# Keys and queries of two batches loaded eight tokens to a partition, and what follows for their use

## The chip, the cores and the metric

The kernel runs on one core of a Trainium2 chip. The core has a matrix engine (TensorE, PE in the profile, with its weight loads as PEld), a vector engine (VectorE, DVE), a scalar engine (ScalarE, ACT), GpSimd (POOL) and a sync engine (SP) that here only issues transfers. Sixteen DMA engines move data. SBUF is the on-chip memory of 128 partitions, PSUM the one that matrix results go to. The metric is the device time of one execution in microseconds (us); lower is better.

## The reference

A sparse attention of 4 batches, 8 heads, 768 tokens and 64 numbers to a head, followed by two matrix products with a gated activation between them. Cut to what matters:

```python
k_sum = k.reshape(B, H, nb, block, D).max(axis=3)      # block = 32, nb = 24
v_sum = v.reshape(B, H, nb, block, D).mean(axis=3)
scores_l = scale * np.matmul(q, k.transpose(0, 1, 3, 2))
mask_l = np.abs(pos[:, None] - pos[None, :]) < window  # window = 16
scores_s = scale * np.einsum('bhsd,bhnd->bhsn', q, k_sum) + np.log(block)
a = softmax(np.concatenate([where(mask_l, scores_l, -1e9), scores_s], axis=-1))
x = np.matmul(a, np.concatenate([v, v_sum], axis=2))   # then heads side by side: 3072 x 512
h = x @ w_in                                           # 512 x 2048
out = (h / (1 + exp(-beta * h))) @ w_out               # 3072 x 512
```

A token thus looks at some 31 neighbours and at one summary (a maximum of keys, a mean of values) for each of 24 blocks.

## The kernel before

The order of work is written out by hand: every engine executes its instructions in the order of the program, and the planner is a small list in which "main" steps on TensorE have "side" steps set between them at given positions (`run`, with pairs of position and function). Batch 0 has a path of its own. For each of batches 1 to 3, the scores and the weighted sums are computed during the output product of the batch before, and the loads and layouts for it during the hidden product and the output product of the batch before.

The eight heads go in four pairs g. A pair's two heads lie in partitions 0 to 63 and 64 to 127 of the transposed tiles. For each batch and pair:

- `kT[g]`: keys transposed, 128 partitions (2 heads x 64 numbers) by tokens, with 16 zero columns at either end. `qn[g]`: queries in the same way, without the zeros.
- `kw[g]`: twelve windows, one for each tile of 64 queries, of 128 columns: 96 neighbouring keys, then the 24 block maxima. It is the stationary operand of the scores.
- `km[g]`: the block maxima, copied by POOL into each window (`key_sums`, L237).
- The scores (L307) take for every tile and head 64 query columns of `qn` as the moving operand. ScalarE makes the exponentials (L316), VectorE or POOL multiplies by the mask (L320), TensorE multiplies with values (L395), VectorE divides (L422), and ScalarE issues a DMA transpose of the result to `xT` (L447).

How keys and queries come into these layouts differs by batch. Batches 0 and 1 are loaded by POOL's queue with a cast to bf16, eight tokens to a partition (CS, L44), into `krow` and `qrow` (96 rows); TensorE transposes them (L256), and copies out of PSUM (L240, L243) put the tokens in order. There, block c of 96 columns holds the tokens 8r + c. For batch 1 the window copy (`windows_perm`, L216) reads with a step, and the maximum is taken from the windows (`key_max_win`, L228).

Batches 2 and 3 go another way, all issued by SP. `hw_load` (L87, DMA at L90) brings a pair's 384 KB of f32 into a staging tile, token 128 j + p in partition p, so that each packet is one token's 64 numbers, 256 B. POOL casts it to bf16 (`kq_cast`, L453 to L456) into a tile of a pool of its own, `natp`. SP issues a DMA transpose (`kq_dma`, L465 to L468) into `kT` or `qn`, tokens in order. VectorE then copies the windows from `kT` (`windows_nat`, L225) and takes the maximum from `kT` (`key_max_nat`, L232). The values take the same sort of way (`load_v`, L94; `v_cast`, L324; `v_odd_dma`, L335), and their block means come from a product with `A_avg` (`vm_all`, L369).

The positions of these steps are in the last loop of the kernel (L708 to L752). SP's queue holds, for a batch, in this order: two query loads (behind the stores of the output product that ends there), then key transposes with the other query loads between them, value loads, query transposes, the two DMAs per pair for the values, and the key loads for the next batch. An instruction in that queue that waits holds all behind it.

Of the kernel before, what the change touches and what calls it, by code (L numbers as in the profile page):

```python
# [11 lines left out]
def kernel(  # L12
# [10 lines left out]
    nc = tc.nc  # L23
    ctx.enter_context(tc.manual_schedule())
    P = 128
    f32 = mybir.dt.float32
    bf16 = mybir.dt.bfloat16
# [4 lines left out]
    B, H, S, D = q.shape  # L32
    block = 32
    W = 16
    nb = S // block
    QT = 64
    NT = S // QT
    HT = NT // 2
    HS = S // 2
    J6 = S // P  # L40
    JV = 2 * J6 + 1
    G = H // 2
    NK = QT + 2 * W
    CS = (8, 8)  # L44
    scale = 1.0 / math.sqrt(D)
    log_block = math.log(block)
    d_model = moe_w_in.shape[0]
# [6 lines left out]

    const = ctx.enter_context(tc.tile_pool(name="consts", bufs=1))
    stage = ctx.enter_context(tc.tile_pool(name="stage", bufs=4))
    natp = ctx.enter_context(tc.tile_pool(name="nat", bufs=4))
    ep = ctx.enter_context(tc.tile_pool(name="ep", bufs=8))
    xp = ctx.enter_context(tc.tile_pool(name="xp", bufs=4))
    op = ctx.enter_context(tc.tile_pool(name="op", bufs=3))  # L60
# [7 lines left out]
    def pair(a, b, g):  # L68
        return a[b, 2 * g:2 * g + 2]


    stg = {}
    loads = {}

    krow = const.tile([P, H // 2 * 16 * D], bf16, name="krow")
    qrow = const.tile([P, H // 2 * 16 * D], bf16, name="qrow")
    def row_view(t, b, lo, hi):
        c = CS[b]
        r = S // c
        hs = H // (2 if 2 * r <= P else 1)  # L80
        p0 = lo // hs * QT
        return t[p0:p0 + r].rearrange("p (h e) -> p h e", e=c * D)[:, lo % hs:lo % hs + hi - lo]

    def sw_load(t, src, b, lo, hi):
        return nc.gpsimd.dma_start(out=row_view(t, b, lo, hi), in_=src[b, lo:hi].rearrange("h (p c) d -> p h (c d)", c=CS[b]))

    def hw_load(nm, src, b, g):  # L87
        f = stage.tile([P, 2, J6, D], f32, name=nm + "st", tag=nm + "st")
        stg[(nm, b, g)] = f
        nc.sync.dma_start(out=f[:], in_=pair(src, b, g).rearrange("h (j p) d -> p h j d", p=P))  # L90

    vst = [const.tile([P, JV, D], f32, name=f"vst{g}") for g in range(G)]

# [38 lines left out]
    kw = [const.tile([P, NT, P], bf16, name=f"kw{g}") for g in range(G)]  # L132
# [3 lines left out]
    kT = [const.tile([P, S + 2 * W], bf16, name=f"kT{g}") for g in range(G)]  # L136
# [47 lines left out]
    qn = [const.tile([P, S], bf16, name=f"qn{g}") for g in range(G)]  # L184
# [28 lines left out]
    def strided(a, dims):  # L213
        return bass.AP(a.tensor, a.offset, [list(a.ap[0])] + dims)

    def windows_perm(cp, g, src, C):  # L216
        R, F, FW = S // C, QT // C, W // C
        t = kw[g][:, :, 0:NK].rearrange("p m (f c) -> p m f c", c=C)
        cs = src.ap[1][0]
        cp(t[:, 1:NT - 1], strided(src[:, :, F - FW:], [[F, NT - 2], [1, F + 2 * FW], [cs, C]]))  # L220
        e = kw[g][:, 0, W:NK]
        cp(strided(e, [[(NT - 1) * P - W, 2], [C, F + FW], [1, C]]),
           strided(src[:, :, 0:1], [[R - F - FW, 2], [1, F + FW], [cs, C]]))

    def windows_nat(cp, g):  # L225
        cp(kw[g][:, :, 0:NK], strided(kT[g][:, 0:1], [[QT, NT], [1, NK]]))

    def key_max_win(g):  # L228
        nc.vector.tensor_reduce(out=km[g][:, NK:NK + nb].rearrange("p (m n) -> p m n", n=2),  # L229
                                in_=kw[g][:, :, W:W + QT].rearrange("p m (n f) -> p m n f", f=block), op=ALU.max, axis=AX.X)  # L230

    def key_max_nat(g):  # L232
        nc.vector.tensor_reduce(out=km[g][:, NK:NK + nb], in_=kT[g][:, W:W + S].rearrange("p (n f) -> p n f", f=block),  # L233
                                op=ALU.max, axis=AX.X)
# [13 lines left out]
    def turned(row, b, t, g):  # L248
        C = CS[b]
        R = S // C  # L250
# [8 lines left out]
    def kt0(g, bg, cp, km=True):  # L259
        t = turned(krow, 0, big[bg], g)  # L260
        cp(kT[g][:, W:W + S].rearrange("p (f c) -> p f c", c=CS[0]), t.rearrange("p c f -> p f c"))
        if km:
            key_max_nat(g)

    def kt_pe(b, g, bg, cp):
        windows_perm(cp, g, turned(krow, b, big[bg], g), CS[b])

# [4 lines left out]
    def qt_pe(b, g, bg, cp):  # L272
        t = turned(qrow, b, big[bg], g)
        cp(qn[g].rearrange("p (f c) -> p f c", c=CS[b]), t.rearrange("p c f -> p f c"))


    et = {}

    def q_tile(g, h, m):
        return qn[g][h * D:(h + 1) * D, m * QT:(m + 1) * QT]  # L280

    def scores0(g, u, bg, pe=True):
        s = big[bg]
# [18 lines left out]
    def scores(b, g, u, bg):  # L302
        s = big[bg]
        for j in range(HT):
            m = u * HT + j
            for h in range(2):
                nc.tensor.matmul(s[:, h, j * QT:(j + 1) * QT], kw[g][h * D:(h + 1) * D, m, :], q_tile(g, h, m),  # L307
                                 start=True, stop=True)
        weigh(b, g, u, s)
        if g < G - 1 or b == 1:  # L310
            mask_e(b, g, u)
# [136 lines left out]
                                    in_=xn[(b, g)].rearrange("p j h d -> p (j h d)"))  # L448


    nat = {}

    def kq_cast(eng, nm, b, g):  # L453
        t = natp.tile([P, J6, 2, D], bf16, name=nm + "n", tag=nm + "n")
        nat[(nm, b, g)] = t
        return eng.tensor_copy(out=t[:], in_=stg[(nm, b, g)].rearrange("p h j d -> p j h d"))  # L456

    last_mask = {}

    def key_cast(n, g):  # L460
        i = kq_cast(nc.gpsimd, "k", n, g)
        if g == 0 and n - 1 in last_mask:
            behind(i, last_mask[n - 1])

    def kq_dma(nm, b, g):  # L465
        t = kT[g][:, W:W + S] if nm == "k" else qn[g][:]
        nc.sync.dma_start_transpose(out=t.rearrange("p (j t) -> p j t", j=J6),
                                    in_=nat[(nm, b, g)].rearrange("p j h d -> p (j h d)"))  # L468


    def h_begin(i, t, lo, hi):
# [150 lines left out]
    s = []  # L622
    wo = []

    def scale4(p, eng=None):
        for n in range(4 * p, 4 * p + 4):
            scale_w_out(n, eng)
# [26 lines left out]
    s = [(6, lambda: scale4(1)), (12, lambda: scale4(2)), (.5, clear_kw)]  # L654
# [5 lines left out]

    def load_keys(n):
        for g in range(G):
            hw_load("k", k, n, g)


    def scores_at(b, s, pos):
# [24 lines left out]
    s = [(.05, exp_table), (.15, lambda: scale4(3)), (.7, lambda: km_pe(2, nc.gpsimd)), (2.9, lambda: km_pe(3, nc.gpsimd))]  # L691
# [16 lines left out]
    for b in range(1, B):  # L708
        n = b + 1
        s = []  # L710
        if n < B:
            for g in range(2):
                s.append((0 + .1 * g, lambda g=g, n=n: hw_load("q", q, n, g)))
            for g in range(G):
                s.append((.5 + g, lambda g=g: key_cast(n, g)))
                s.append((.6 + g, lambda g=g: kq_dma("k", n, g)))
                s.append((3.5 + g, lambda g=g: windows_nat(dve_cp, g)))
                s.append((3.6 + g, lambda g=g: key_max_nat(g)))
                s.append((4.7 + g, lambda g=g: kq_cast(nc.gpsimd, "q", n, g)))
                s.append((8 + g, lambda g=g: key_sums(nc.gpsimd, g)))  # L720
                s.append((6.6 + 1.5 * g, lambda g=g: kq_dma("q", n, g)))
                s.append((12.6 + 1.2 * g, lambda g=g: v_cast(nc.gpsimd, g)))
                s.append((12.7 + 1.2 * g, lambda g=g: v_odd_dma(g)))
            for g in range(2):
                s.append((.7 + g, lambda g=g, n=n: hw_load("q", q, n, g + 2)))
                s.append((2.7 + g, lambda g=g: load_v(n, g)))
                s.append((6.7 + 1.5 * g, lambda g=g: load_v(n, g + 2)))
        if n + 1 < B:
            for g in range(G):
                s.append(((16.31, 16.32, 19.3, 19.31)[g], lambda g=g, n=n: hw_load("k", k, n + 1, g)))  # L730
        late = [x for x in s if x[0] >= 16]
        run([lambda i=i: h_tile(i) for i in range(k2)], [x for x in s if x[0] < 16])
        s = [((x[0] - 16) * 1.2, x[1]) for x in late]
        if n < B:
            scores_at(n, s, [1, 5.9, 8, 10.1])
            av_at(n, s, [10.2, 13.1, 13.2, 13.3], [0, 1, 2, 0])
            for g in range(G):
                s.append(((10.3, 13.35, 13.4, 13.5)[g], lambda g=g: x_dma(n, g)))
            s.append((5.99, lambda: vm_all(big[0], VMC)))
            s.append((6.3, lambda: spread(0)))  # L740
            s.append((8.3, lambda: spread(1)))
        main = [lambda ms=ms, a=a: o_atom(b, ms, a) for ms in range(J6 - (n == B)) for a in range(4)]
        run(main, s)
        if n == B:
            ms = J6 - 1
            for lo, hi in ((0, 256), (256, 512)):
                t = one[0 if lo else 1][:, 0]
                for kk in range(k2):
                    o_mm(ms, kk, t, lo, hi)
                o = op.tile([P, hi - lo], f32, name="o_half", tag=f"o_half{lo}", bufs=1)  # L750
                nc.vector.tensor_copy(out=o[:], in_=t[:, 0:hi - lo])
                nc.sync.dma_start(out=out_r[b * J6 + ms][:, lo:hi], in_=o[:])  # L752
# [29 lines left out]
```

## Time and profile before

| | |
|---|---|
| median of 3 runs | 216.02 us (215.3 to 217.65) |
| profiled execution | 217.07 us, its span 215.3 us |
| TensorE clock granted | 1.000 |
| TensorE busy | 207.2 us |
| VectorE, ScalarE, POOL busy | 99.1, 107.7, 57.5 us |
| DMA packets | 85287, of them 73728 under 512 B |
| key loads of batches 2 and 3 (8) | 384 KB each, 5.4 us to landing |
| query loads of batches 2 and 3 (8) | 384 KB each, 4.1 us to landing |
| key and query transposes (8 and 8) | 4.3 and 4.1 us to landing |
| hidden product for batch 1's x, with the loads for batch 2 | 78.2 to 98.8 us |
| output product, with the scores of batch 2 | 98.8 to 124.2 us |
| hidden product for batch 2's x, with the loads for batch 3 | 124.2 to 145.0 us |
| output product, with the scores of batch 3 | 145.0 to 170.3 us |

Times within the profile are counted from the first instruction of the profiled execution. A group of instructions is told by line, engine, operation, what it writes and reads, partitions by elements, and number; then its busy time in us and the mean of one in ns; then the idle time of its engine just before it, and what ended most of that idle time. Waits are told as who waited for whom: us in total, times, longest. The chain of waits is the chain of work that ended last, with start, length and what ran.

### The profile page before, as it was taken

What the parts mean: (1) busy time and instruction counts of PE and PEld (TensorE: products, weight loads), DVE (VectorE), ACT (ScalarE), POOL (GpSimd) and SP (SyncE); (2) the same over time, 40 slices, a digit from 0 to 9 for tenths busy, and PEclk for the clock granted to TensorE, in tenths of its full rate; (3) what the DMA queues carried; (4) which work ended last, traced back from release to release, by engine and by line L of the source; (5) the groups of instructions that cost most, each with busy time, mean ns of one, the idle gap of its engine ahead of it and who ended that gap; (6) DMA issues with size and microseconds to landing.
All of it is one profiled execution on the core that took longest, in us unless ns stands there. A gap on an engine that the chain in (4) does not pass through costs nothing.

```text
span 215.3 us, 5346 instructions
## 1 busy us (share of the span) xinstructions
PE 207.2 (96%) x2242; PEld 121.0 (56%) x2242; DVE 99.1 (46%) x233; ACT 107.7 (50%) x143; POOL 57.5 (27%) x91
## 2 busy tenths in 40 slices
PE   7789999999999999999999999999999999999993
PEld 7567756665546445665455455654564556654452
DVE  5567766597786612530599212422796200002121
ACT  2258595777676007776681046676660077650000
POOL 7946990010517403441105004433000000000000
PEclk9999999999999999999999999999999999999999
DMA  6999999999949999999699979999527400001212
GB/s 118 181 212 161 191 175 198 206 209 191 225 114 226 269 199 236 230 195 159 147 215 214 247 184 227 180 200 196 136 70 182 120 24 0 0 3 49 97 49 97
DMA packets 85287, 34.09 MB, mean 158 GB/s; under 512 B 73728, under 2 KB 82320, under 8 KB 85264
## 3 DMA queue, kind: packets, MB, share of 16 engines
q1 hardware_dynamic: 68192, 24.05, 55.3%
q0 software_dynamic: 7440, 7.34, 21.3%
q10 hardware_dynamic: 9632, 2.37, 7.6%
q8 instruction: 17, 0.28, 0.6%
q14 instruction: 6, 0.05, 0.1%
HBM read 27.37 MB, written 6.29 MB: 156 GB/s over the span
## 4 chain that ended last, share of the span: by engine, by line
PE 87%; DMA 6%; DVE 3%; issue 1%; ACT 0%; POOL 0%; POOLq 0%; DVEq 0%
PE one L505 36%; PE big L487 29%; PE big L473 5%; PE one L479 3%; DMA xT<-xn 3%; DMA krow<-in_k_dram 3%; PE big L256 3%; PE big L307 3%; PE big L395 2%; PE big L479 2%; DVE xn L422 1%; DVE qn L243 1%; PE big L294 1%; PE big L286 1%; PE big L369 1%
## 5 line engine op out<-in xcount | busy, mean ns | idle before, releaser
L505 PE MATMUL one<-w_out_sb,h_sb 128*128 128x512 bf16 (+1 forms) x400 | 86.3, 371 | 0.0
L500 ACT ACTIVATE h_sb<-big,beta_sb 128x768 bf16<-128x768 f32 x48 | 42.7, 901 | 52.5 <-PE big L487 52.5
L487 PE MATMUL big<-xT,w_in_sb 128*128 128x384 bf16 x384 | 63.0, 326 | 0.3 <-DMA xT<-xn 0.3
L505 PEld LDWEIGHTS <-h_sb 128*128 128x128 bf16 x400 | 37.8, 98 | 40.9 <-issue 0.2
L487 PEld LDWEIGHTS <-w_in_sb 128*128 128x128 bf16 x384 | 37.6, 98 | 25.6 <-issue 0.5
L243 DVE COPY o_sb<-one 128x512 f32<-128x512 f32 x20 | 13.8, 688 | 47.4 <-PE one L505 47.3
L316 ACT ACTIVATE e<-big,bias 128x768 bf16<-128x768 f32 x32 | 27.1, 899 | 7.5 <-PE big L307 4.9
L320 DVE TENSOR_TENSOR e<-e,mask 128x768 bf16<-128x768 bf16 x24 | 14.2, 618 | 19.0 <-ACT e L316 18.9
L325 POOL CAST ve<-vst 128x832 bf16<-128x832 f32 x15 | 13.2, 889 | 9.8 <-DMA vst<-in_v_dram 9.7
L243 DVE COPY kw<-kT 128x1152 bf16<-128x1152 bf16 x8 | 4.0, 496 | 22.5 <-DMA kT<-kn 22.5
L456 POOL CAST qn<-qst 128x768 bf16<-128x768 f32 x8 | 6.6, 830 | 28.7 <-DMA qst<-in_q_dram 28.7
L237 POOL COPY kw<-km 128x288 bf16<-128x288 bf16 x12 | 5.5, 471 | 27.6 <-DVE km L229 21.7
L422 DVE TENSOR_TENSOR xn<-big,r 128x768 bf16<-128x768 f32 (+1 forms) x14 | 12.6, 900 | 0.5
L233 DVE TENSOR_REDUCE km<-kT 128x24 bf16<-128x768 bf16 x12 | 11.2, 943 | 2.4 <-ACT kT L240 2.4
L473 PE MATMUL big<-xT,w_in_sb 128*128 128x384 bf16 x64 | 11.4, 326 | 0.0
L456 POOL CAST kn<-kst 128x768 bf16<-128x768 f32 x8 | 6.5, 828 | 13.8 <-DVE e L320 11.4
L620 ACT ACTIVATE h_sb<-big,beta_sb 128x384 bf16<-128x384 f32 x16 | 8.1, 580 | 2.7 <-PE big L473 2.7
L522 PE MATMUL one<-blank 128*128 128x128 bf16 (+1 forms) x105 | 7.2, 231 | 1.3 <-DVE blank L118 1.3
L479 PEld LDWEIGHTS <-w_in_sb 128*128 128x128 bf16 x64 | 6.1, 98 | 4.0
L479 PE MATMUL one<-xT,w_in_sb 128*128 128x384 bf16 x44 | 8.1, 326 | 0.0
L473 PEld LDWEIGHTS <-w_in_sb 128*128 128x128 bf16 x64 | 5.9, 98 | 3.5
L395 PEld LDWEIGHTS <-e 128*64 128x64 bf16 x336 | 6.2, 111 | 2.1 <-issue 1.6
(122 smaller groups left out, 187.8 us busy)
## 6 DMA issues: line engine op xcount, KB each, us to landing
out_dram<-o_sb SPq DMA_DIRECT2D x23, 256.0 KB, 2.5
vst<-in_v_dram SPq DMA_DIRECT2D x13, 336.0 KB, 4.6
kst<-in_k_dram SPq DMA_DIRECT2D x8, 384.0 KB, 5.4
qst<-in_q_dram SPq DMA_DIRECT2D x8, 384.0 KB, 4.1
w_in_sb<-in_moe_w_in_dram POOLq DMA_DIRECT2D x4, 512.0 KB, 6.1
w_out_sb<-in_moe_w_out_dram POOLq DMA_DIRECT2D x4, 512.0 KB, 14.2
vo<-ve SPq DMA_DIRECT2D x12, 107.2 KB, 2.3
vst<-in_v_dram SPq DMA_DIRECT2D x3, 416.0 KB, 6.8
```

Source lines behind the costliest of these rows:

```text
L233: nc.vector.tensor_reduce(out=km[g][:, NK:NK + nb], in_=kT[g][:, W:W + S].rearrange("p (n f) -> p n f", f=block), op=ALU.max, axis=AX.X)
L243: nc.vector.tensor_copy(out=o, in_=i)
L316: return nc.scalar.activation(out=e[:], in_=s[:, :, 0:HS], func=ACTF.Exp, bias=bias[:, 0:1], scale=scale)
L320: return (nc.gpsimd if (b, g) == (1, G - 1) else nc.vector).tensor_mul(out=e.rearrange("p h (m q) -> p h m q", q=QT), in0=e.rearrange("p h ...
L325: eng.tensor_copy(out=ve[:, g, lo:hi, 0:D], in_=vst[g][:, lo:hi])
L422: nc.vector.tensor_mul(out=x[:, 3 * us[0]:3 * us[0] + 3 * n].rearrange("p (k j) h d -> p k (j h) d", k=n), in0=tv[:, :, :, 0:D], in1=r[:, ...
L456: return eng.tensor_copy(out=t[:], in_=stg[(nm, b, g)].rearrange("p h j d -> p j h d"))
L473: nc.tensor.matmul(t[:, 0:HS], w_in_sb[:, ki, i * P:(i + 1) * P], xT[:, ki, 0:HS], start=(ki == 0), stop=(ki == k1 - 1))
L479: nc.tensor.matmul(t[:, 0:HS], w_in_sb[:, ki, i * P:(i + 1) * P], xT[:, ki, lo:lo + HS], start=(ki == 0), stop=(ki == k1 - 1))
L487: nc.tensor.matmul(t[:, kk, 0:HS], w_in_sb[:, ki, i * P:(i + 1) * P], xT[:, ki, kk * HS:(kk + 1) * HS], start=(ki == 0), stop=(ki == k1 - 1))
L500: nc.scalar.activation(out=h_sb[:, i, :].rearrange("p (k m) -> p k m", k=2), in_=t[:, :, 0:HS], func=ACTF.Silu, scale=beta_sb[:, i:i + 1])
L505: nc.tensor.matmul(t[:, 0:hi - lo], h_sb[:, n, ms * P:(ms + 1) * P], w_out_sb[:, n, lo:hi], start=(n == 0), stop=(n == k2 - 1))
```

## The change

Keys and queries of batches 2 and 3 are loaded eight tokens to a partition (CK = 8, RK = 96 rows), so that a packet is 2 KB. The casts write into `krow` and `qrow`, the tiles of batch 1's loads, and the pool `natp` goes. For keys the casts of pairs 1 and 3 are VectorE's, those of pairs 0 and 2 POOL's; queries stay with POOL. The DMA transposes take 8 blocks of 96 rows instead of 6 of 128, and leave the tokens in the order in which batch 1's lie: block c of 96 columns holds the tokens 8r + c. `kT` is written from column 0. The window copy is then `windows_perm`, two copies that read with a step of 96 numbers, and the maximum is taken from the windows. For queries nothing puts the tokens in order: the tile's 64 columns are read by the score product with a stride.

In the order of each engine's instructions: TensorE's, ScalarE's, POOL's and SP's stay where they were, but that POOL loses two casts a batch. VectorE's gets, where four pairs of window copy and maximum stood, this: cast of pair 1; two copies of pair 0; cast of pair 3; maximum of pair 0; and then two copies and a maximum for each other pair.

```diff
+    CK = 8
+    RK = S // CK
...
-    natp = ctx.enter_context(tc.tile_pool(name="nat", bufs=4))
...
-    def hw_load(nm, src, b, g):
-        f = stage.tile([P, 2, J6, D], f32, name=nm + "st", tag=nm + "st")
+    def row_load(nm, src, b, g):
+        f = stage.tile([RK, 2, CK * D], f32, name=nm + "st", tag=nm + "st")
         stg[(nm, b, g)] = f
-        nc.sync.dma_start(out=f[:], in_=pair(src, b, g).rearrange("h (j p) d -> p h j d", p=P))
+        nc.sync.dma_start(out=f[:], in_=pair(src, b, g).rearrange("h (p c) d -> p h (c d)", c=CK))
...
-    def q_tile(g, h, m):
-        return qn[g][h * D:(h + 1) * D, m * QT:(m + 1) * QT]
+    def q_tile(g, h, m, b=0):
+        r = slice(h * D, (h + 1) * D)
+        if b < 2:
+            return qn[g][r, m * QT:(m + 1) * QT]
+        F = QT // CK
+        return strided(qn[g][r, m * F:m * F + 1], [[1, F], [RK, CK]])
...
-    nat = {}
+    def nat_view(nm, g):
+        return {"k": krow, "q": qrow}[nm][0:RK, g * CK * 2 * D:(g + 1) * CK * 2 * D]
 
     def kq_cast(eng, nm, b, g):
-        t = natp.tile([P, J6, 2, D], bf16, name=nm + "n", tag=nm + "n")
-        nat[(nm, b, g)] = t
-        return eng.tensor_copy(out=t[:], in_=stg[(nm, b, g)].rearrange("p h j d -> p j h d"))
+        t = nat_view(nm, g).rearrange("p (c h d) -> p c h d", c=CK, h=2)
+        return eng.tensor_copy(out=t, in_=stg[(nm, b, g)].rearrange("p h (c d) -> p c h d", c=CK))
...
+    KC = [nc.gpsimd, nc.vector, nc.gpsimd, nc.vector]
 
     def key_cast(n, g):
-        i = kq_cast(nc.gpsimd, "k", n, g)
+        i = kq_cast(KC[g], "k", n, g)
...
     def kq_dma(nm, b, g):
-        t = kT[g][:, W:W + S] if nm == "k" else qn[g][:]
-        nc.sync.dma_start_transpose(out=t.rearrange("p (j t) -> p j t", j=J6),
-                                    in_=nat[(nm, b, g)].rearrange("p j h d -> p (j h d)"))
+        t = kT[g][:, 0:S] if nm == "k" else qn[g][:]
+        nc.sync.dma_start_transpose(out=t.rearrange("p (j t) -> p j t", j=CK),
+                                    in_=nat_view(nm, g))
...
-                s.append((3.5 + g, lambda g=g: windows_nat(dve_cp, g)))
-                s.append((3.6 + g, lambda g=g: key_max_nat(g)))
+                s.append((3.5 + g, lambda g=g: windows_perm(dve_cp, g, kT[g][:, 0:S].rearrange("p (c r) -> p c r", c=CK), CK)))
+                s.append((3.6 + g, lambda g=g: key_max_win(g)))
```

The two copies of a pair's windows, whose code is not changed:

```python
    def windows_perm(cp, g, src, C):
        R, F, FW = S // C, QT // C, W // C
        t = kw[g][:, :, 0:NK].rearrange("p m (f c) -> p m f c", c=C)
        cs = src.ap[1][0]
        cp(t[:, 1:NT - 1], strided(src[:, :, F - FW:], [[F, NT - 2], [1, F + 2 * FW], [cs, C]]))
        e = kw[g][:, 0, W:NK]
        cp(strided(e, [[(NT - 1) * P - W, 2], [C, F + FW], [1, C]]),
           strided(src[:, :, 0:1], [[R - F - FW, 2], [1, F + FW], [cs, C]]))
```

## The prediction, made before the changed kernel was run

> **What bounds the kernel now.** I read the page's busy line and its 40 slices first, then the waits of TensorE, the chain of waits, and last the windows of the stages that the change touches.
>
> ```profile
> PE 207.2 (96%) x2242; PEld 121.0 (56%) x2242; DVE 99.1 (46%) x233; ACT 107.7 (50%) x143; POOL 57.5 (27%) x91
> ...
> PE   7789999999999999999999999999999999999993
> ...
> DMA  6999999999949999999699979999527400001212
> ```
>
> TensorE is busy 96% of the span, and the missing part lies in the first slices and the last one. The DMA engines are nearly full until about 155 us. Whether that fullness costs anything is told by what TensorE waits for:
>
> ```profile
> PE big L256 <- DMA krow<-in_k_dram: 1.4, 2, 1.0
> PE one L522 <- DVE blank L118: 1.3, 1, 1.3
> PE big L286 <- DVE qn L243: 0.7, 2, 0.4
> PE big L256 <- ACT kT L240: 0.6, 1, 0.6
> PE big L487 <- DMA xT<-xn: 0.3, 1, 0.3
> PE big L403 <- DVE vm_one L243: 0.2, 1, 0.2
> ```
>
> All but the one at L487 belong to the first 26 us, in batch 0, which the change leaves alone. After that TensorE waits once, 0.3 us, for a transposed xT. The windows of the two batches that are changed say the same (columns: length, busy time of each engine with its number of instructions, clock, DMA share, GB/s):
>
> ```profile
> 78.20:98.80 20.60, 20.59 (x127) 12.42 (x127) 5.65 (x9) 13.34 (x15) 6.95 (x11) 1.00 1.23 217
> 98.80:124.20 25.40, 25.40 (x319) 12.70 (x317) 14.80 (x31) 10.95 (x14) 4.82 (x6) 1.00 1.07 198
> 124.20:145.00 20.80, 20.80 (x129) 12.52 (x128) 6.00 (x9) 13.35 (x15) 6.81 (x10) 1.00 1.16 197
> 145.00:170.30 25.30, 25.30 (x317) 12.66 (x316) 15.09 (x31) 10.96 (x14) 1.76 (x2) 1.00 0.67 146
> ```
>
> The reader is to see that TensorE has no hole here. So a faster load cannot buy more than the 0.3 us, and anything that makes a TensorE instruction longer is paid in full. The chain shows the instructions whose operand changes:
>
> ```profile
> 100.57 0.46 PE big L307 x24
> ...
> 104.59 0.46 PE big L307 x24
> ...
> 108.25 0.46 PE big L307 x24
> ...
> 110.54 0.46 PE big L307 x24
> ```
>
> **The change part by part.** The profiled execution took 217.07 us, a span of 215.3 and 1.8 around it; it lies 1.05 us above the median of 216.02. The sum is made against 217.07 and then shifted by 1.05.
>
> *Loads.* Sixteen loads (4 pairs of heads, keys and queries, two batches) of 384 KB go from 1536 packets of 256 B to 192 of 2 KB. A packet of queue q1 takes on average 55.3% x 215.3 us x 16 engines / 68192 packets = 28 ns, so one load holds all 16 engines for 1536 x 28 / 16 = 2.7 us. What a 2 KB packet takes lies between the same 28 ns (0.3 us a load) and eight times that (2.7 us, no gain); I take the middle, 1.5 us. The key loads for batch 2 are issued from 62.8 to 67.8 us and run beside the transposes of batch 1's x, which end last before the 0.3 us wait (xT landed 2.8 to 7.7 us after issue). Without that company xT comes before TensorE asks: -0.3 us. If loads gain nothing, 0. Everything else that the loads speed up ends at TensorE instructions that run without a hole: nothing.
>
> *Transposes.* Before: 128 rows of 6 blocks of 128 numbers; after: 96 rows of 8 such blocks. Both are 768 blocks of 256 B. Sixteen issues stay where they were in SP's queue. I take nothing; if their landing (3.5 to 5.0 us) grew by a third, cover is from the last query transpose issue at 101.6 us to the scores of pair 3 at 110.5.
>
> *Casts.* POOL casts took 8 x 0.83 = 6.6 us a batch. Now POOL does 6 of 1024 columns instead of 768, 6 x 0.83 x 1024/768 = 6.6 us, and DVE does 2, each by its cast of vst (832 columns, 1008 ns) 1.24 us. They add waits. On DVE the cast of pair 1 stands behind the o_sb copy at 77.62 and is due at SP's second kT transpose (83.47): 4 us of cover. That of pair 3 stands behind the first window copy, which waits for kT; it would end at 85.03 + 1.34 + 1.24 = 87.6, and SP issues the fourth kT transpose at 89.29: 1.7 us of cover. Behind that transpose SP holds the v loads and the query transposes. krow and qrow were last read by TensorE at 46.7 and 56.3 us and are written from 69 and 82 us on: nothing.
>
> *Windows.* The copy of kw from kT was one of 1152 columns, unit stride; it becomes 960 + 160 columns read with a step of 96 bf16 numbers (192 B).
>
> ```profile
> L243 DVE CAST kw<-big 128x960 bf16<-128x960 f32 x4 | 4.6, 1148 | 2.5 <-PE big L256 2.5
> ...
> L243 DVE COPY kw<-kT 128x1152 bf16<-128x1152 bf16 x8 | 4.0, 496 | 22.5 <-DMA kT<-kn 22.5
> ...
> L233 DVE TENSOR_REDUCE km<-kT 128x24 bf16<-128x768 bf16 x12 | 11.2, 943 | 2.4 <-ACT kT L240 2.4
> ```
>
> The first row has the very shape and a step too, though out of PSUM; the timeline has four of them (two pairs) in 2.68 us, 1.34 us a pair, against 0.50. The maximum stays (941 ns from kw, 943 from kT). DVE gains 4 x 0.84 + 2 x 1.24 = 5.8 us a batch, in a stage where it is busy 5.65 of 20.6 us. A pair then costs 1.34 + 0.94 = 2.3 us, less than the 2.6 to 3.3 us between two kT landings, so the last maximum ends about 1 us later than 94.5, and the scores that need it come at 110.5: nothing. Bounds: 0.50 us as before, and 2.4 us a pair at the slowest rate of any elementwise row (POOL's mask product, 768 columns in 1640 ns, 2.1 ns each); even so POOL's last cast of v would end at 103.6, before TensorE asks at 104.97 (the working is in the third rival).
>
> *Query tiles.* 192 score matmuls (4 pairs x 2 halves x 6 tiles x 2 heads, batches 2 and 3) now read their 64 moving columns one number per 192 B. No row of this trace shows TensorE doing so. Contiguous, 384 columns take 20.80 us / 128 = 163 ns, 0.426 ns each, so 64 take 27 ns; 24 matmuls take 0.46 us, 38 ns for the two heads of a tile, which must therefore run beside each other (two in a row would be 55). Lower bound: nothing; a gain is excluded, since the columns are as many. The nearest rows are ACT and DVE fetching separated numbers: ACT's strided copies (kT, 768 columns, 799 ns) against its plain ones (o_sb, 512, 587 ns) give 0.83 ns a column, DVE's rows (960 at 1148 ns, 160 at 310) give 1.05. Upper bound: 1.05 ns and no overlap of the heads, 192 x 64 x (1.05 - 0.43) = +7.7 us. I take the faster of the two rates, 0.83 ns, with the heads beside each other: 96 x 64 x (0.83 - 0.43) = +2.5 us.
>
> The Trainium skill, Advanced Engine Details and Errata, section SBUF Cachelines, says that SBUF is read in 16-byte lines and that an access pattern needs at least two hits on a line for full speed. It speaks against the change, for here each number has its own line; at half rate, an estimate of mine from that page, it would add 96 x 27 ns = 2.6 us, against nothing if stride were free. No run here shows it yet.
>
> **Sum:** 217.07 - 0.3 + 2.5 = 219.3, and less 1.05: **218.2 us**, 1.0% above the median.
>
> **The rivals.** *Free stride (not slower).* TensorE takes strided columns at 0.426 ns. For it: DVE and ACT rows with a step out of PSUM cost what plain ones cost. Against it: those engines ask for a number only every 0.83 to 1.05 ns, half TensorE's rate. It decides wherever a separate number comes within 0.43 ns. 216.02 - 0.3 = 215.7 us.
>
> *Heads in a row or slower fetches.* If both heads' reads contend, 192 x 64 x 0.40 = +5.0 us, 220.7; with 1.05 ns 223.4. For it: nothing shows that two strided reads overlap. Against it: the contiguous ones do.
>
> *Late windows.* If DVE needs over twice 1.34 us for the strided copies of a pair, w, the wait moves: DVE's last maximum, then POOL's copy (0.43) and its four casts of v (4 x 0.88), which L369 on TensorE needs at 104.97. From kT's landing at 85.03: 85.03 + 1.24 + 4 x (w + 0.94) + 0.43 + 3.52 passes 104.97 at w = 2.75 us. At w = 2.9 it waits 0.6 us there and, from 131.79, 1.2 us at 151.19 in batch 3: +1.8, 220.0 us with the forecast's other terms. For it: no row shows DVE hopping in SBUF. Against it: the bound above was 2.4 us, PSUM's step costs DVE nothing, and kT will land earlier. The Trainium skill's Vector Engine (DVE) Microarchitecture Reference, section 5.2, has hops at every element at 1.73 to 2.50 ns; w would be about 2.0 to 2.9 us by that, an estimate, and no run here shows it.
>
> *The loads don't get shorter.* Then only the 0.3 us is missing: 218.5 us.
>
> **How the numbers follow.** Stride at about 0.83 ns, including loads that gain nothing: 0.37. Free stride: 0.33. Contention or slower: 0.19. Late windows: 0.08. Something outside these that is faster by over 1%: 0.03; it would need 2.2 us from a TensorE that shows 0.3 us of holes. Three runs of this kernel spread over 1%, so 1% is about what a measurement tells from no change. The forecast sits on that border: of its 0.37 I count 0.24 slower and 0.13 within, the other slow cases 0.27 slower, free stride 0.32 within and 0.01 faster: faster 0.04, same 0.45, slower 0.51. The range goes from free stride less 0.4 us of spread, 215.3, to nearly the upper bound of the query term, 223.0; outside stay the faster case and part of the contention, some 0.1 to 0.15.
>
> **What would show it.** Loads: about 192 packets each, q1's packets down by 16 x 1344 = 21,504, landing under 4 us. Query tiles: the chain's pieces of 24 score matmuls in batches 2 and 3 at about 0.8 us instead of 0.46, with batch 1's unchanged; at 0.46 the forecast falls to 215.7. Windows: DVE's 960-column row near 1.1 us; above 2.3 us, look for a TensorE wait at the A_avg matmuls. The wait for xT gone. What would make it wrong altogether is a TensorE wait after 78 us that none of these steps names.

## The result, and the profile after

The changed kernel takes 223.36 us (median; 222.8 to 223.77), the kernel before 216.25 us: a ratio of 1.0329, 95% interval 1.0296 to 1.0362. It is slower by 7.1 us, against 2.2 forecast, and lies 0.4 us above the range.

The busy line of the page of the changed kernel, with its packets and its queue q1:

```profile
PE 212.9 (96%) x2226; PEld 127.7 (58%) x2242; DVE 107.8 (49%) x245; ACT 107.6 (48%) x143; POOL 59.8 (27%) x87
...
DMA packets 63783, 34.09 MB, mean 154 GB/s; under 512 B 49152, under 2 KB 57744, under 8 KB 63760
...
q1 hardware_dynamic: 46688, 24.05, 48.8%
```

TensorE is still busy 96% of a span that is longer: time was not lost in waiting. (The trace lacks 16 of TensorE's 2242 matmul records, all of the output product, so its busy time here is a little too low.) The packets fell as the change says, by 68192 - 46688 = 21,504 on q1. Which work grew stands in the chain of waits of the changed kernel (start, length, what ran; first batch 1's scores, then two pairs of batch 2's and the hidden products, then two pairs of batch 3's):

```profile
60.89 0.46 PE big L309 x24
...
77.09 20.80 PE big L490 x128
...
99.62 1.41 PE big L309 x24
...
104.59 1.41 PE big L309 x24
...
127.07 20.80 PE big L490 x128
...
149.59 1.42 PE big L309 x24
...
154.57 1.41 PE big L309 x24
...
177.05 20.80 PE big L490 x128
```

The 24 score matmuls of a pair take 1.41 us in place of 0.46 where the query columns are read with a stride, and 0.46 still in batch 1, where they are not. Eight pairs make 8 x 0.95 = 7.6 us. The starts of the hidden products give a ruler that leaves out the first 77 us: from one to the next it is 127.07 - 77.09 = 49.98 us and 177.05 - 127.07 = 49.98 us. Before, the chain has

```profile
78.21 20.64 PE big L487 x126
...
124.19 20.80 PE big L487 x128
...
170.34 20.80 PE big L487 x128
```

which is 45.98 and 46.15; the first is short because that piece begins behind the wait for xT and two matmuls late (x126). So a batch costs 3.83 us more than 46.15, and four pairs at 0.955 make 3.82: nothing is left over for anything else in the change.

The groups by form say the same of the score matmuls of batches 1 to 3 (line, engine, operation, shapes, number, busy us, mean ns, idle before). In the kernel before:

```profile
L307 PE MATMUL big<-qn,kw 64*128 64x64 bf16 x288 | 6.3, 191 | 0.0
```

In the changed kernel, 7.7 us more, with the other edited instructions:

```profile
L309 PE MATMUL big<-qn,kw 64*128 64x64 bf16 x288 | 14.0, 252 | 0.1
...
L458 POOL CAST qrow<-qst 96x1024 bf16<-96x1024 f32 x8 | 8.7, 1097 | 29.2 <-DMA qst<-in_q_dram 29.2
L241 DVE COPY kw<-kT 128x960 bf16<-128x960 bf16 x8 | 8.4, 1044 | 12.4 <-DMA kT<-krow 12.4
...
L241 DVE COPY kw<-kT 128x160 bf16<-128x160 bf16 x8 | 3.0, 375 | 0.0
L458 DVE CAST krow<-kst 96x1024 bf16<-96x1024 f32 x4 | 2.7, 677 | 0.0
```

VectorE's strided window copies take 10.7 us for eight pairs by the page's group, 1.34 us each, and VectorE waits for kT before them, as it did. They are not the bound.

### The profile page after: what moved, and what is told of

Same layout as the page of the kernel before. It is cut to its first block, busy times and chain, and to the rows that moved or that the text cites. A ratio compares the mean times of both kernels' runs of the same rounds, so it can differ in the third digit from the quotient of the medians.

```text
span 222.1 us, 5347 instructions
## 1 busy us (share of the span) xinstructions
PE 212.9 (96%) x2226; PEld 127.7 (58%) x2242; DVE 107.8 (49%) x245; ACT 107.6 (48%) x143; POOL 59.8 (27%) x87
## 3 DMA queue, kind: packets, MB, share of 16 engines
q1 hardware_dynamic: 46688, 24.05, 48.8%
## 4 chain that ended last, share of the span: by engine, by line
PE 89%; DMA 3%; issue 2%; POOL 2%; DVE 2%; ACT 1%; POOLq 0%; DVEq 0%
PE one L508 36%; PE big L490 28%; PE big L309 6%; PE big L476 5%; PE one L482 3%; DMA qrow<-in_q_dram 3%; PE big L254 2%; PE big L397 2%; PE big L482 2%; POOL e L322 1%; DVE qn L241 1%; PE big L296 1%; PE big L288 1%; PE big L371 1%; POOL krow L86 1%
## 5 line engine op out<-in xcount | busy, mean ns | idle before, releaser
L508 PE MATMUL one<-w_out_sb,h_sb 128*128 128x512 bf16 (+1 forms) x384 | 83.8, 370 | 1.8 <-issue 1.4
L490 PEld LDWEIGHTS <-w_in_sb 128*128 128x128 bf16 x384 | 37.6, 98 | 25.1
L322 DVE TENSOR_TENSOR e<-e,mask 128x768 bf16<-128x768 bf16 x24 | 13.4, 571 | 23.8 <-ACT e L318 23.7
L241 DVE COPY kw<-kT 128x960 bf16<-128x960 bf16 (+1 forms) x16 | 10.7, 710 | 12.4 <-DMA kT<-krow 12.4
L458 POOL CAST qrow<-qst 96x1024 bf16<-96x1024 f32 x8 | 8.7, 1097 | 29.2 <-DMA qst<-in_q_dram 29.2
L235 POOL COPY kw<-km 128x288 bf16<-128x288 bf16 x12 | 7.6, 645 | 27.4 <-DVE km L227 26.6
L309 PE MATMUL big<-qn,kw 64*128 64x64 bf16 x288 | 14.0, 252 | 0.1
L309 PEld LDWEIGHTS <-kw 64*128 64x128 bf16 x288 | 11.3, 104 | 4.4 <-issue 4.2
L227 DVE TENSOR_REDUCE km<-kw 128x24 bf16<-128x768 bf16 x12 | 11.3, 947 | 0.2
L482 PEld LDWEIGHTS <-w_in_sb 128*128 128x128 bf16 x64 | 6.1, 98 | 4.0
L458 POOL CAST krow<-kst 96x1024 bf16<-96x1024 f32 x4 | 4.1, 1038 | 15.5 <-DVE e L322 14.8
```

Source lines behind the costliest of these rows:

```text
L241: nc.vector.tensor_copy(out=o, in_=i)
L322: return (nc.gpsimd if (b, g) == (1, G - 1) else nc.vector).tensor_mul(out=e.rearrange("p h (m q) -> p h m q", q=QT), in0=e.rearrange("p h ...
L458: return eng.tensor_copy(out=t, in_=stg[(nm, b, g)].rearrange("p h (c d) -> p c h d", c=CK))
L482: nc.tensor.matmul(t[:, 0:HS], w_in_sb[:, ki, i * P:(i + 1) * P], xT[:, ki, lo:lo + HS], start=(ki == 0), stop=(ki == k1 - 1))
L490: nc.tensor.matmul(t[:, kk, 0:HS], w_in_sb[:, ki, i * P:(i + 1) * P], xT[:, ki, kk * HS:(kk + 1) * HS], start=(ki == 0), stop=(ki == k1 - 1))
L508: nc.tensor.matmul(t[:, 0:hi - lo], h_sb[:, n, ms * P:(ms + 1) * P], w_out_sb[:, n, lo:hi], start=(n == 0), stop=(n == k2 - 1))
```

## The experiments

Each kernel is the changed one with the edit shown, unless it says otherwise. Some read other queries than the reference does; what is left out stands in each expectation. The kernels of runs, steps and heads were executed once each (218.44, 220.7 and 220.19 us); they are read by their pieces, not by their times.

### The stride undone, and the stride alone

```diff
-        F = QT // CK
-        return strided(qn[g][r, m * F:m * F + 1], [[1, F], [RK, CK]])
+        return qn[g][r, m * QT:(m + 1) * QT]
```

> The changed kernel with one thing undone: the score products of batches 2 and 3 read 64 neighbouring query columns again, so they meet queries in another order than the reference (the order is left out, the amount of work is the same). If the stride is the whole cost: the pieces of 24 score matmuls go from 1.41 us back to 0.46, eight of them give back 7.6 us, and the time is about 215.8 us. If the rest of the change (strided window copies, casts on VectorE, transposes of 96 rows) costs something too, the time stays above 217.5.

215.81 us, 0.9988 of the kernel before (0.9958 to 1.0017). Its chain of waits:

```profile
77.65 20.80 PE big L489 x128
...
100.18 0.46 PE big L308 x24
...
123.80 20.80 PE big L489 x128
...
169.95 20.80 PE big L489 x128
```

The pieces are back at 0.46 us, and a batch takes 46.15 us both times, what the kernel before took for its second. All the rest of the change (packets, casts, transposes, window copies) costs and gains nothing there.

The counterpart takes the kernel before and adds the stride alone:

```diff
-    def q_tile(g, h, m):
-        return qn[g][h * D:(h + 1) * D, m * QT:(m + 1) * QT]
+    def q_tile(g, h, m, b=0):
+        r = slice(h * D, (h + 1) * D)
+        if b < 2:
+            return qn[g][r, m * QT:(m + 1) * QT]
+        return strided(qn[g][r, m * 8:m * 8 + 1], [[1, 8], [96, 8]])
```

> The kernel before, with nothing changed but that the 64 query columns of batches 2 and 3 are read with a step of 96 numbers (192 B), so that other queries than the reference's are taken. If the stride is the whole cost: pieces of 24 at 1.41 us, 216.2 + 7.6 = 223.8 us. If half of it came from tiles that lie elsewhere or from DMA traffic of the new loads: pieces under 1.2 us and a time under 221.

223.81 us, 1.0344 of the kernel before (1.031 to 1.0378): 7.6 us more, with no other part of the change in it. Its chain has the same pieces, two of them here:

```profile
100.00 1.41 PE big L310 x24
...
104.97 1.41 PE big L310 x24
```

So the stride of the query tiles is the cause, and within the spread of the runs it is the whole cause. The 7.1 us between the medians of the change are 0.5 less than these 7.6; whether the rest of the change gains a little in the first 77 us is neither shown nor excluded by the interval of 0.9958 to 1.0017.

### What in the stride costs: runs, and steps

The same 64 queries of a tile, read in runs of 1, 2, 4 and 8 neighbours for pairs 0 to 3:

```diff
-        return strided(qn[g][r, m * F:m * F + 1], [[1, F], [RK, CK]])
+        n = (1, 2, 4, 8)[g]
+        return strided(qn[g][r, m * F:m * F + 1], [[n, F // n], [RK, CK], [1, n]])
```

> The changed kernel, with the same 64 queries of a tile read in another order: runs of 1, 2, 4 and 8 neighbouring columns for pairs 0, 1, 2 and 3 (the order of the queries is left out). If each separate fetch costs a fixed time and the columns within a run come with it (16-byte lines): pieces of 24 at 1.41, about 0.9, and 0.46 to 0.5 us for runs of 4 and 8. If the hop itself costs (a restart for each run): 1.41, 0.94, 0.70, 0.58. If any pattern that is not one run falls to a slow mode: 1.41 for all of them.

The four pairs of batch 2 in its chain of waits, in the order of the pairs:

```profile
99.40 1.42 PE big L310 x24
...
104.37 0.77 PE big L310 x24
...
108.35 0.46 PE big L310 x24
...
110.64 0.46 PE big L310 x24
```

Runs of 4 and 8 are free, runs of 2 add a third of what single columns add (0.77 us, where about 0.9 was expected). That is not a slow mode for all patterns, nor a restart for each run: 16 runs of 4 cost nothing. Between 64 and 32 runs lie 1.42 - 0.77 = 0.65 us for 12 tiles of two heads, 0.65 / 12 / 32 = 1.7 ns for each separate fetch; 16 fetches, at 1.7 ns, are 27 ns and no longer than the 64 columns themselves (163 / 384 = 0.42 ns each, 64 x 0.42 = 27 ns).

A constant step tells a fetch of neighbours from a fetch of a line of 16 bytes:

```diff
-        return strided(qn[g][r, m * F:m * F + 1], [[1, F], [RK, CK]])
+        n = (None, None, (2, 4, 8, 10), (1, 3, 6, 9))[b][g]
+        return strided(qn[g][r, m * F:m * F + 1], [[n, QT]])
```

> The changed kernel with the 64 query columns of a tile read at a constant step (other queries than the reference's are taken): batch 2, pairs 0 to 3, steps of 2, 4, 8 and 10 numbers (4, 8, 16, 20 bytes); batch 3, pairs 0 to 3, steps of 1, 3, 6 and 9. Theory A with lines of 16 bytes (a fetch of 1.65 ns brings a line, and all columns in it): a piece of 24 takes 0.46 us at steps 1 and 2, 0.6 at 3, 0.77 at 4, 1.1 at 6, and 1.41 at 8, 9 and 10. Theory A with neighbours only (what isn't adjacent is a fetch of its own): 1.41 for every step from 2 on.

The chain of waits from 98 to 165 us, batch 2 with steps of 2, 4, 8 and 10 numbers, then batch 3 with 1, 3, 6 and 9:

```profile
99.83 0.46 PE big L310 x24
...
103.84 0.81 PE big L310 x24
...
107.86 1.48 PE big L310 x24
...
111.17 1.51 PE big L310 x24
...
148.41 0.46 PE big L310 x24
...
152.43 0.66 PE big L310 x24
...
156.28 1.15 PE big L310 x24
...
159.26 1.52 PE big L310 x24
```

A step of 2 numbers is free, though no two columns are neighbours, so it is not adjacency. The cost follows the number of 16-byte lines that 64 columns touch: 16 at step 2, 24 at 3, 32 at 4, 48 at 6 and 64 from 8 on, with 0.46, 0.66, 0.81, 1.15 and 1.5 us. In the change's order the 64 columns of a tile lie on 8 such lines, 8 neighbouring columns on each (on 16, if `qn` does not begin on a line), but every column lies on another line than the one read just before it, and the price is that of 64 lines. So what counts is each move to another line: a line that was left is paid for again eight columns later. At steps of 8 to 10 a piece takes up to 0.1 us more than at the change's step of 96; the cause of that stays open.

### Do the two heads contend?

The stride for some heads only, and in batch 3's first two pairs all tiles of one head before the other's:

```diff
+        jh = [(j, h) for j in range(HT) for h in range(2)]
+        hop = (True, True)
+        if b == 2:
+            hop = ((True, True), (True, False), (False, True), (False, False))[g]
+        if b == 3:
+            hop = ((True, True), (False, False), (True, True), (False, False))[g]
+            if g < 2:
+                jh = [(j, h) for h in range(2) for j in range(HT)]
```

> The changed kernel with the strided read for some heads only; where it is not strided, other queries than the reference's are met. Batch 2: pair 0 both heads strided, pair 1 the first head only, pair 2 the second only, pair 3 none. Batch 3: pairs 0 and 1 take all six tiles of one head and then of the other (0 strided, 1 not), pairs 2 and 3 tile by tile as before (2 strided, 3 not). Theory A, a strided column takes 1.65 ns and the heads run beside each other: one strided head costs as much as two, 1.41 us a piece in batch 2's pairs 1 and 2, and head after head costs about twice, 2.6 us, in batch 3's pair 0. Theory B, a strided column takes 0.83 ns and the two heads' reads go one after the other: one strided head costs about half of the addition, 0.9 us, and head after head stays near 1.4.

The chain of waits from 97 to 165 us: batch 2's four pairs, then batch 3's. The number behind the x counts what the chain passes through, not all that ran (each of batch 2's pieces stands with x24 in the timeline).

```profile
98.61 1.42 PE big L316 x24
103.59 1.41 PE big L316 x15
...
108.20 1.42 PE big L316 x16
111.46 0.46 PE big L316 x24
...
147.64 1.62 PE big L316 x22
152.82 0.53 PE big L316 x24
...
156.56 1.42 PE big L316 x24
159.80 0.46 PE big L316 x24
```

One strided head costs as much as two, whichever it is. If the heads' reads went one after the other, half of the matmuls contiguous would have saved nearly half of the addition. So the heads run beside each other, and the slower sets the pace. The second part of the test did not separate the theories: head after head takes 1.62 us, neither 2.6 nor 1.4. The single records of that piece show why: the starts form two interleaved series, each 100 to 110 ns apart, so TensorE overlapped the two heads' tiles although the program names six of one and then six of the other.

### Two ways to keep the rest of the change

Keys by the change, queries by the old way:

```diff
-                s.append((0 + .1 * g, lambda g=g, n=n: row_load("q", q, n, g)))
+                s.append((0 + .1 * g, lambda g=g, n=n: hw_load("q", q, n, g)))
...
     def kq_dma(nm, b, g):
+        if nm == "q":
+            nc.sync.dma_start_transpose(out=qn[g][:].rearrange("p (j t) -> p j t", j=J6),
+                                        in_=nat[(nm, b, g)].rearrange("p j h d -> p (j h d)"))
+            return
```

> The change for keys alone; queries of batches 2 and 3 are loaded, cast and transposed as in the kernel before and read contiguously. If nothing but the stride of the query tiles costs: pieces of 24 at 0.46 us, 215.8 us, within 0.3% of the kernel before. If the keys' part costs through VectorE or SP's queue: above 217.

215.73 us, 0.9973 of the kernel before (0.9949 to 0.9997). The interval just leaves out 1. Its chain:

```profile
76.84 20.80 PE big L505 x128
...
122.98 20.80 PE big L505 x128
...
169.13 20.80 PE big L505 x128
```

A batch takes 46.14 and 46.15 us, the same as before. What it is ahead, it is ahead by 77 us, in a stretch where the kernel before itself starts its first hidden product at different times (below). I don't count it as a gain.

The whole change, with eight neighbours (16 bytes) to a run and the exponential putting the columns in order:

```diff
-        return strided(qn[g][r, m * F:m * F + 1], [[1, F], [RK, CK]])
+        return strided(qn[g][r, m * F:m * F + 1], [[RK, CK], [1, F]])
...
+        if b > 1:
+            for h in range(2):
+                nc.scalar.activation(out=e[:, h].rearrange("p (m f c) -> p m f c", m=HT, c=CK),
+                                     in_=s[:, h, 0:HS].rearrange("p (m c f) -> p m f c", m=HT, c=CK),
+                                     func=ACTF.Exp, bias=bias[:, 0:1], scale=scale)
```

> The whole change, but a tile's 64 queries are read as 8 runs of 8 neighbours (16 bytes), and the exponential puts them back in order: it reads the scores with a step and is split into one instruction per head for batches 2 and 3. If a run of 8 costs TensorE nothing: pieces of 24 at 0.46 us. The exponentials become 2 x 0.58 us instead of 0.90, 16 x 0.26 = 4.2 us more on ScalarE, which has room: 215.8 us, as the kernel with contiguous reads. If a step in the write of the exponential slows ScalarE to twice: 2 x 0.9 us for each half, and the scores wait for their buffers, 218 us or more.

216.57 us, 1.0022 of the kernel before (0.9994 to 1.005): 6.8 us of the 7.1 are back. ScalarE's steps cost nothing that shows: 581 ns for 384 columns, against 579 ns for its activation of 384 columns without a step in the hidden product (another function). But the chain of waits now goes through ScalarE ahead of the second half of the last pair's scores; by the order of the program these are written to a PSUM tile that ScalarE has yet to read:

```profile
107.38 0.48 PE big L309 x24
...
107.97 2.00 ACT e L320 x4
...
110.02 0.35 PE big L309 x12
```

A batch takes 0.26 us longer than 46.15 in that kernel (its hidden products start at 77.13, 123.56 and 169.95 us).

### Is the 0.3 us wait for xT one of the loads?

The kernel before, unchanged, for two more profiles:

> The kernel before, unchanged, for a second profile. Question: does TensorE wait for xT at the start of the hidden product of batch 1's x in every execution? If the wait belongs to the loads of 256 B packets, as the prediction's term of -0.3 us has it, the 0.3 us are there again. If it comes and goes with the execution, it is absent or of another size.

> The kernel before once more, for a third profile: as the second, a wait of about 0.3 us for xT if it belongs to the loads, none or another size if it comes and goes.

216.09 and 215.93 us. Neither waits for xT; the chain of the first one, whose hidden product starts 1.0 us earlier than in the profile that the prediction read, has:

```profile
70.71 6.46 DMA xT<-xn
77.21 20.64 PE big L487 x126
```

The chain still comes by way of the transposes there, but TensorE was not kept waiting. The kernel before with the stride alone, which keeps the old loads, shows no such wait either.

## Why the prediction was wrong, point by point

**What bounds the kernel: right.** TensorE without a hole after 26 us, a longer TensorE instruction paid in full, nothing to win from faster loads. The batch of 46.15 us with and without the rest of the change is the proof.

**Query tiles: the term that failed, in its size.** "I take the faster of the two rates, 0.83 ns, with the heads beside each other: 96 x 64 x (0.83 - 0.43) = +2.5 us." The heads do run beside each other. But a column on another 16-byte line than the column before it takes about 1.7 ns, not 0.83, so the term is 8 x 0.95 = 7.6 us. The flaw was to take the rate at which ScalarE and VectorE fetch separated numbers for a rate of TensorE's reads. Those rows come from PSUM and from engines that take one column in 0.83 and 1.05 ns anyway; they put no floor or ceiling on TensorE. With 7.6 in its place the sum is 217.07 - 0.3 + 7.6 = 224.4, less 1.05: 223.3 us, and 223.36 was measured.

With the -0.3 left out, which was not the change's (below), it is 223.6: both lie within the spread of the runs.

The bound of +7.7 held the term by luck. It stood for two heads in a row at 1.05 ns, and neither is so. It was also not the bound of its own case: it takes 0.43 ns off each of 192 matmuls, though the kernel before pays for 96, since its heads overlap. Worked out with that, heads in a row at 1.05 ns are 192 x 64 x 1.05 - 96 x 64 x 0.43 = +10.3 us. And the range ended at 223.0, below 223.4, the time that the prediction itself gave for that bound.

**The 16-byte lines.** The Trainium skill's rule (Advanced Engine Details and Errata, SBUF Cachelines) holds as to what counts: the cost follows the lines of 16 bytes, and reads of one line help each other only when they follow one another. The rule's figure does not hold: two hits on a line are not enough here (runs of 2: 0.77 us, step 4: 0.81 us, against 0.46); four are (step 2, or runs of 4: 0.46). And a single hit runs at a quarter of full speed (1.7 against 0.42 ns), not at my estimate of half. The prediction's "here each number has its own line" is not exact: up to eight numbers of a tile share a line, but they are not read one after the other.

**Loads: right in the packets, wrong in the 0.3 us.** q1's packets cost 55.3% x 215.3 x 16 = 1905 engine-us before and 48.8% x 222.1 x 16 = 1734 after; all of it put down to the 16 loads and spread over 16 engines, the saving is 0.67 us a load, where I took 1.2. Landing got hardly shorter for keys (5.4 to 5.1 us) and longer for queries (4.1 to 4.8); "under 4 us" was wrong. Queries land in 4.6 to 4.9 us in all six kernels with the new query load, and in 4.1 to 4.2 in the five profiles with the old one; why, no run shows. The wait for xT is gone in the changed kernel, but it is gone in two of three profiles of the kernel before as well, and in that of the stride alone with the old loads. The term was read from one execution, and belonged to that execution.

**Transposes, casts, windows: right.** In the stage from 78 to 100 us, transposes land in 4.8 and 4.1 us against 4.1 and 4.4. VectorE's cast took 677 ns, not 1.24 us, and POOL's 1.04 to 1.1 against 1.11; their waits delayed nothing that TensorE needed. A pair's windows took 1.34 us, as estimated, and the last maximum ended at 94.0 us against 94.5 before; counted from the starts of the hidden product above (77.09 and 78.21) that is 0.6 us later, where I took about 1.

**The rivals.** Free stride fell with the first trace. Heads in a row was right in that it came out far slower, but the mixed pairs rule out its mechanism. Its price was also too low by its own logic, since it left out the overlap that would have been lost: at 0.83 ns it would be 192 x 64 x 0.83 - 96 x 64 x 0.43 = +7.6 us. The time alone thus could not tell it from what happened; the pairs with one strided head do. That its 223.4, for 1.05 ns, lies next to the measured time is luck. Late windows fell: the Trainium skill's Vector Engine (DVE) Microarchitecture Reference, section 5.2, has 1.73 to 2.50 ns for hops at every element, measured there on 4-byte words and a program with two sources. Here the bf16 copy of 960 columns at 192 B steps took 1044 ns, 1.1 ns a column, and a pair's windows 1.34 us, far from the 2.75 us at which TensorE would have waited.

## What to carry to other kernels

Where TensorE is the bound, the access pattern of its moving operand is a cost of its own: let at least four bf16 columns that are read one after the other come from one 16-byte line (measured here for tiles of 64 columns), or put the order right on an engine with room. When no row shows an operation on the engine in question, another engine's row is not its price; let the range reach the time of the bound, and a little past it. A wait that stands once in one profile, and is as small as the spread between runs, is not yet a term of a sum.

## What the runs showed that I had not expected

- TensorE and VectorE both slow down at a step of 192 B in SBUF, but not alike. TensorE goes from 0.42 to 1.7 ns a column, VectorE's bf16 copy from 0.43 (496 ns for 1152) to 1.1 (1044 ns for 960).
- Eight columns that share a 16-byte line are no help when seven others are read between them: the change's tiles, on 8 or 16 lines, cost 1.41 us a piece, and steps of 8 to 10 numbers, on 64 lines, 1.5.
- A contiguous head beside a strided one does not help at all: 1.41 us for the pair, as with both strided.
- TensorE overlapped the tiles of two heads that the program had put six apart: 0.53 us for 24 contiguous matmuls head after head, where 24 x 27 ns without overlap would be 0.65.
